# Decay attention with two expert layers on one core: another order of the steps in a chunk, and attention products in fp32

## The chip, the core and the metric

The kernel runs on one core of a Trainium2 chip. The core has five engines that run side by side, each with its own queue: TensorE (PE, matrix products; its weight loads are shown as PEld), VectorE (DVE), ScalarE (ACT), GpSimd (POOL) and SyncE (SP, which here only issues transfers). SBUF is the working memory with 128 partitions, PSUM the memory that products are written to. The metric is the device time of one execution in microseconds.

## What is computed

Three layers follow one another. The attention keeps, for each of 4 x 8 heads, a complex state of 48 x 48, which decays row by row at each of 768 steps and takes up k v. Its result goes through a dense layer of eight experts (weighted by a Sinkhorn-normalised gate) and then a layer in which each token goes to one expert.

```python
def _attn_ref(q, k, v, a_re, a_im):
    mag = np.sqrt(a_re * a_re + a_im * a_im)
    scale = np.minimum(mag, 0.999) / (mag + 1e-06)
    a_re_n, a_im_n = (a_re * scale, a_im * scale)
    for t in range(S):                      # 768 steps, B, H, D = 4, 8, 48
        ar, ai = (a_re_n[:, :, t, :, None], a_im_n[:, :, t, :, None])
        new_re = ar * S_re - ai * S_im
        new_im = ar * S_im + ai * S_re
        S_re, S_im = (new_re + k_t v_t, new_im)
        y[:, :, t] = einsum('bhd,bhde->bhe', q[:, :, t], S_re)

def _moe_ref(x, ...):   # 3072 tokens of 384; P: Sinkhorn of exp(x @ w_gate)
    for e in range(8):
        out += P[:, e:e + 1] * (np.maximum(x @ w1[e], 0.0) @ w2[e])

def _moe2_ref(x, ...):  # every token through its best expert, times the gate
    out[mask] = gate_w[mask, None] * (np.maximum(x[mask] @ w1[e], 0.0) @ w2[e])
```

## The kernel before

**Tiles.** A tile n is a chunk of 128 steps of one batch: n = chunk * 4 + batch, 24 tiles. In the attention the decays lie with (head, row) on the partitions and the steps along the free dimension, three planes of 128 steps per tile. `prep` makes the cumulated products of decays within the chunk for two tiles at once (`L = 2`; the first two tiles singly). It normalises the decays (`decay`), then scans. The 128 steps are taken as 16 runs of 8. For j = 1 to 7 step j of every run is multiplied with step j - 1: one product L233 of all four real and imaginary parts, then a difference L235 and a sum L236. Element j of all runs is a strided view, eight elements apart. Then the ends of the 16 runs are combined by doubling (L244 to L246), and these prefixes are multiplied into the other steps (L252 to L254). Squares, Ln and Exp on ACT give the inverse magnitudes, and L273 and L275 write q times the product and k over the product into `WW`.

**A tile's attention.** `stack` brings `WW` by ten transfers on SP's queue into `QK`, real part on partitions 0 to 47, imaginary part on 64 to 111. `tile_attn` makes the scores (PE, L351, fp32), masks and scales them (DVE, L355), splits them into a high and a low fp16 part (ACT L357, POOL L358), transposes K (L365, L366) and makes y of 48 fp16 products (L374): per head three with the scores and v, and from the second chunk on three with q and the state, both of which are split before (ACT L342 and L344, POOL L343, DVE L345). Powers of two for these splits come from sums of squares of q, k and v (`scales`, L303 to L317). The state is updated after U (L381): twelve small copies on ACT (L388 to L390) gather each slot's decay of the whole chunk into `C`, DVE adds the old state (L395), ACT swaps halves (L396, L397), and POOL multiplies and adds (L401 to L403).

**x.** `emit_x` scales y by a power of two from its row's largest magnitude, splits it (L421, L422), transposes it on PE (L426) and copies it to `xg` (ACT, L429). Then follow its logits (L440).

**The first two experts.** `tile_unit` runs expert 0 and 1 on pairs of tiles: zt (L506), relu and split (L527 on ACT, L528 on DVE), yt (L517), and `evac_raw` (L533 on ACT, transfer L534 on POOL's queue).

**What sets the order.** In the first phase the order on PE is written out by hand: `tile_attn` yields between its pieces and `step` puts pieces of `tile_unit` between them. The other engines' orders come from a scheduler. Products of attention share three PSUM buffers (tag "ps"), z's and zt's three, the expert outputs two. After the first phase come a dense stage on six further experts (L471, L482) and the routed stage.

## Time and profile before

| | us |
|---|---|
| runs of the kernel before | 2189.81, 2195.47, 2196.0 (median 2195.47) |
| profiled execution, span | 2188.0 |
| of it, to the first dense product after the first phase (L471) | 782.3 |
| PE busy over the span | 1962.5 (90%) |
| DVE busy over the span | 1357.6 (62%) |
| ACT busy | 903.9 (41%) |
| POOL busy | 367.1 (17%) |

The profile is one execution. Busy time is the union of an engine's instructions; an instruction may start before the one ahead of it has ended. PEclk is the granted clock of PE as a share of 2.4 GHz. "idle before" is the time in which an engine did nothing before such instructions, and after the arrow stands what ended it. The share over the whole span mixes a first phase, in which attention runs, with a long stage of plain products, so the stretches have to be read apart.

### The profile page before, as it was taken

Reading aid. Unit: us, or ns where it says so; the run is one execution under the profiler, and the core shown is the slowest. Engines: PE = TensorE matmul, PEld = TensorE weight load, DVE = VectorE, ACT = ScalarE, POOL = GpSimd, SP = SyncE. Lnnn points to the kernel's source line nnn. Section 1 sums busy time; section 2 is a strip of 40 time slices with the busy share of each in tenths; the row PEclk is TensorE's granted clock in tenths of the full one; section 3 lists DMA queues with packets and bytes.
Section 4 is the critical chain, followed back from the end, with each engine's and each line's share of the span. In section 5 each row is a group of like instructions: output and inputs, shape, how many; then the busy total and the mean of one; then the engine's idle time right before and its main releaser. Section 6 shows DMA issues by size and latency. Waiting matters only on the chain.

```text
span 2188.0 us, 37978 instructions
## 1 busy us (share of the span) xinstructions
PE 1962.5 (90%) x14770; PEld 1258.3 (58%) x14770; DVE 1357.6 (62%) x2826; ACT 903.9 (41%) x1816; POOL 367.1 (17%) x408
## 2 busy tenths in 40 slices
PE   1468878788888999999999999999999999989997
PEld 1356656666666655555555555555555555567885
DVE  8999999999996644334443443443444355554885
ACT  6565555555544433223333332433443133355111
POOL 1213332333332110000110110011011010100005
PEclk9679889999999999999999999999999999999999
DMA  4222222222222251001330231133023300143222
GB/s 159 69 81 78 80 73 81 81 81 81 81 66 73 81 189 55 29 1 58 116 116 30 87 116 58 58 116 116 29 87 116 144 25 20 38 131 130 111 89 88
DMA packets 66779, 181.53 MB, mean 83 GB/s; under 512 B 9827, under 2 KB 50799, under 8 KB 61472
## 3 DMA queue, kind: packets, MB, share of 16 engines
q0 software_dynamic: 19264, 96.19, 12.6%
q1 hardware_dynamic: 47328, 82.80, 12.6%
q8 instruction: 123, 2.02, 0.4%
q14 instruction: 64, 0.52, 0.1%
HBM read 114.09 MB, written 46.63 MB: 73 GB/s over the span
## 4 chain that ended last, share of the span: by engine, by line
PE 51%; issue 9%; POOL 1%; DMA 1%; DVE 1%; ACT 0%; POOLq 0%; SPq 0%; DVEq 0%
PE ym L482 25%; PE z L471 25%; POOL out_dram L831 1%; DMA out_dram<-ya,tok 0%; DMA late<-srt 0%; PE pt L602 0%; DVE h L528 0%; ACT h L527 0%; POOL srt L663 0%; PE pl L440 0%; PE wsum L131 0%; PE z L807 0%; DMA srt<-row,posi 0%; ACT xt L604 0%; DVE eq L627 0%
## 5 line engine op out<-in xcount | busy, mean ns | idle before, releaser
L471 PE MATMUL z<-xg,wt 128*128 128x512 f16 x2592 | 570.3, 379 | 3.5 <-ACTq L1168 3.5
L482 PE MATMUL ym<-wt,h 128*128 128x384 f16 x3456 | 572.2, 326 | 0.0
L482 PEld LDWEIGHTS <-h 128*128 128x128 f16 x3456 | 336.7, 98 | 222.3
L528 DVE SCALAR_TENSOR_TENSOR h<-z,h 128x512 f16<-128x512 f32 (+1 forms) x400 | 245.4, 615 | 300.4 <-ACT h L527 295.1
L471 PEld LDWEIGHTS <-wt 128*128 128x128 f16 x2592 | 252.0, 98 | 296.9 <-issue 1.9
L527 ACT ACTIVATE h<-z 128x512 f16<-128x512 f32 (+1 forms) x400 | 213.2, 534 | 432.2 <-PE z L471 305.5
L506 PE MATMUL zt<-xg,wt 128*128 128x256 f16 (+1 forms) x1872 | 223.5, 282 | 41.5 <-ACT xg L429 41.5
L555 DVE SCALAR_TENSOR_TENSOR acc<-ym,pf,acc 128x384 f32<-128x384 f32 x120 | 74.1, 617 | 279.1 <-PE ym L482 279.1
L517 PE MATMUL yt<-wt,ht 128*128 128x384 f16 x1152 | 210.5, 336 | 21.7 <-DVE ht L528 14.9
L506 PEld LDWEIGHTS <-wt 128*128 128x128 f16 x1872 | 183.6, 105 | 70.2 <-issue 43.1
L517 PEld LDWEIGHTS <-ht 128*128 128x128 f16 x1152 | 112.3, 102 | 106.0 <-DVE ht L528 25.7
L807 PE MATMUL z<-x,late 128*128 128x128 f16 x2016 | 131.5, 220 | 7.5 <-DVE late L796 5.1
L807 PEld LDWEIGHTS <-late 128*128 128x128 f16 x2016 | 120.9, 98 | 22.1 <-DVE late L796 6.9
L822 PE MATMUL y<-wq,h 128*128 x672 | 127.4, 327 | 1.7 <-issue 1.5
L108 ACT ACTIVATE wm<-st 128x1024 f32<-128x1024 f32 x48 | 50.7, 1057 | 145.9 <-DMA st<-in_w_dram 144.9
L358 POOL TENSOR_TENSOR sc<-sc,sc 128x512 f16<-128x512 f32 x48 | 62.9, 1311 | 173.4 <-ACT sc L357 172.4
L233 DVE TENSOR_TENSOR T<-A 128x384 f32<-128x384 f32 (+1 forms) x91 | 88.2, 969 | 2.7 <-ACT T L200 1.0
L357 ACT CAST sc<-sc 128x512 f16<-128x512 f32 x48 | 29.6, 617 | 141.7 <-DVE sc L355 141.7
L822 PEld LDWEIGHTS <-h 128*128 128x128 f16 x672 | 61.8, 98 | 33.6 <-issue 4.1
L117 ACT ACTIVATE wm<-st,ws 128x512 f16<-128x512 f32 x96 | 63.7, 713 | 38.9 <-DVE ws L138 38.9
L796 DVE COPY late<-wq 128x1536 f16 x112 | 63.0, 562 | 26.2 <-DVE ya L829 12.4
L762 POOL DMA_DIRECT2D w1d<-wm x64 | 48.0, 755 | 185.5 <-ACT wm L117 184.6
(296 smaller groups left out, 2376.2 us busy)
## 6 DMA issues: line engine op xcount, KB each, us to landing
st<-in_w_dram POOLq DMA_DIRECT2D x31, 1536.0 KB, 7.3
QK<-WW SPq DMA_DIRECT2D x96, 145.1 KB, 3.5
w1d<-wm POOLq DMA_DIRECT2D x64, 192.0 KB, 3.0
w2d<-wm POOLq DMA_DIRECT2D x32, 384.0 KB, 2.9
wq<-w2d SPq DMA_DIRECT2D x4, 3072.0 KB, 10.5
wq<-w1d SPq DMA_DIRECT2D x4, 3072.0 KB, 11.2
a<-in_att_dram SPq DMA_DIRECT2D x24, 384.0 KB, 3.8
qk<-in_att_dram SPq DMA_DIRECT2D x24, 384.0 KB, 4.3
```

The costliest lines, as they stand in the source:

```text
L117: nc.scalar.activation(hi[:, sl], st[:, sl], AF.Copy, scale=s)
L233: tt(out=x, in0=cur[:, None].to_broadcast([P, 2, 2, ns]), in1=pre[:, :, None].to_broadcast([P, 2, 2, ns]), op=ALU.mult)
L471: nc.tensor.matmul(z, w1[:, hw, k, f * P:(f + 1) * P], xg[:, hx, k, :], start=(i == 0), stop=(i == 8))
L482: nc.tensor.matmul(y, hs[f][:, hh, i * P:(i + 1) * P], w2[:, hw, f, :], start=(j == 0), stop=(j == 23))
L506: nc.tensor.matmul(z[:, f], w1[:, hw, k, o:o + P], xg[:, hx, k, :], start=(j == 0), stop=(j == 8))
L517: nc.tensor.matmul(y, hs[f // fz][:, hh, f % fz, i * P:(i + 1) * P], w2[:, hw, f, :], start=(j == 0), stop=(j == 23))
L527: nc.scalar.activation(h[:, 0], z, AF.Relu)
L528: nc.vector.scalar_tensor_tensor(out=h[:, 1], in0=z, scalar=0.0, in1=h[:, 0], op0=ALU.max, op1=ALU.subtract)
L555: self.nc.vector.scalar_tensor_tensor(out=acc, in0=y, scalar=self.pf[:, e, n:n + 1], in1=acc, op0=ALU.mult, op1=ALU.add)
L796: nc.vector.tensor_copy(wc, w1[:, bass.ds(r * 1536, 1536)])
L807: nc.tensor.matmul(z[:, f], wc[:, hw, k, f * P:(f + 1) * P], x[:, hx * 3 + k, :], start=(i == 0), stop=(i == 8))
L822: nc.tensor.matmul(y, h[:, hh, f, :], w2[:, bass.ds(r * 1536 + (hw * 2 + f) * 384, 384)], start=(i == 0), stop=(i == 5))
```

## The change

The 128 steps of a chunk are laid out anew by the host: index j * 16 + s instead of s * 8 + j, for q, k, v and the decays. In the scan, step j of all 16 runs is now one run of 16 neighbours. L233 becomes two instructions (one for each of real and imaginary part of the step before). The mask and the tokens' numbers follow the new order: `time_order` computes them once, and in the routed stage an iota per tile becomes a copy of a column of `tokid`.

The scores stay in fp32 (mask only), as do q, v and the state. So y has per head one fp32 product with the scores and one with the state; the splits, their casts and `scales` with its product fall away.

The state update is on DVE: `UV` holds U plus state and its swapped half side by side, one product with the decays straight from `QK` and one sum take the place of POOL's three instructions and ACT's twelve copies. For that, the last column of K's plane is now written as needed (imaginary part, once with its sign turned).

`emit_x` takes the power of two from the row's sum of squares: a Square with a sum on ACT and four small DVE instructions in place of a reduction and five.

The buffers `q16`, `v16`, `C`, `V`, `bound` fall away. The last pairs' decay uses the buffer `xs`.

```diff
-        v, v16, scl = self.vs.pop(n)
+        v = self.vs.pop(n)
         last = c == NC - 1
-        sc = ap.tile([P, 2, 8, P], F16, name=f"sc{n}", tag="sc")
-        if c > 0:
...
-            nc.scalar.copy(Q16[:, 0], Q[:, :, 0:128])
-            nc.gpsimd.tensor_tensor(out=Q16[:, 1], in0=Q[:, :, 0:128], in1=Q16[:, 0], op=ALU.subtract)
-            nc.scalar.activation(S16[:, 0], self.S[b], AF.Copy, scale=scl[:, 2:3])
-            nc.vector.scalar_tensor_tensor(out=S16[:, 1], in0=self.S[b], scalar=scl[:, 2:3], in1=S16[:, 0], op0=ALU.mult,
-                                           op1=ALU.subtract)
+        sc = ap.tile([P, 8, P], F32, name=f"sc{n}", tag="sc")
...
-                nc.vector.scalar_tensor_tensor(out=sc32, in0=ps, scalar=scl[:, 3:4],
-                                               in1=self.mask[:, None, :].to_broadcast([P, 4, P]), op0=ALU.mult, op1=ALU.mult)
-                nc.scalar.copy(hi, sc32)
-                nc.gpsimd.tensor_tensor(out=lo, in0=sc32, in1=hi, op=ALU.subtract)
+                tt(out=sc[:, g * 4:g * 4 + 4, :], in0=ps, in1=self.mask[:, None, :].to_broadcast([P, 4, P]), op=ALU.mult)
...
         for s in range(8):
-            parts = [(Q16, S16), (sc, v16)] if c > 0 else [(sc, v16)]
-            mm = [(l[:, i, s, :], r[:, j, cols[s]]) for l, r in parts for i, j in ((0, 0), (0, 1), (1, 0))]
-            for i, (l, r) in enumerate(mm):
-                nc.tensor.matmul(y[:, cols[s]], l, r, start=(i == 0), stop=(i == len(mm) - 1))
+            if c > 0:
+                nc.tensor.matmul(y[:, cols[s]], Q[:, s, 0:128], self.S[b][:, own[s]], start=True, stop=False)
+            nc.tensor.matmul(y[:, cols[s]], sc[:, s, :], v[:, cols[s]], start=c == 0, stop=True)
...
-            ut(out=e3(Us), in0=e3(Us), in1=Cb(0), op=ALU.mult)
-            ut(out=e3(V), in0=e3(V), in1=Cb(1), op=ALU.mult)
-            ut(out=self.S[b], in0=Us, in1=V, op=ALU.add)
+            tt(out=e4, in0=e4, in1=self.QK[n % 2][:, :, :, 128:129].to_broadcast([PR, 2, 8, 48]), op=ALU.mult)
+            tt(out=self.S[b], in0=UV[:, 0], in1=UV[:, 1], op=ALU.add)
...
-            tt(out=x, in0=cur[:, None].to_broadcast([P, 2, 2, ns]), in1=pre[:, :, None].to_broadcast([P, 2, 2, ns]),
-               op=ALU.mult)
+            x = T[:, :, :, 0:ns].rearrange("p d c (r s) -> p d c r s", s=16)
+            for d in range(2):
+                tt(out=x[:, d], in0=cur, in1=pre[:, d:d + 1].to_broadcast([P, 2, R, 16]), op=ALU.mult)
...
+        nc.scalar.activation(junk, x, AF.Square, accum_out=ss)
+        ts(out=ss, in0=ss, scalar1=2.0 ** -100, scalar2=None, op0=ALU.max)
+        ts(out=ss.bitcast(I32), in0=ss.bitcast(I32), scalar1=1, scalar2=0x7F800000, op0=ALU.logical_shift_right,
+           op1=ALU.bitwise_and)
+        ts(out=inv, in0=ss, scalar1=2.0 ** (64 - 5), scalar2=None, op0=ALU.mult)
+        nc.vector.reciprocal(out=s, in_=inv)
...
+    step = np.arange(P).reshape(16, 8).T.reshape(P)
+    st = st.reshape(4, B, 3, P, NC, P)[..., step]
```

On VectorE, the start of a pair's scan in the middle of the first phase; A are the decay products, T the scan's scratch, ht and zt belong to an expert on the tiles before. Before:

```order
L528 SCALAR_TENSOR_TENSOR ht_8_0_4089<-zt_8_0_4070,ht_8_0_4089 128x512
L233 TENSOR_TENSOR T_4358<-A_4357 128x4x96
L235 TENSOR_TENSOR A_4357<-T_4358 128x96
L236 TENSOR_TENSOR A_4357<-T_4358 128x96
L433 TENSOR_SCALAR lg<-pl_4125,invsx,wgs 128x8
```

And of the kernel after, whose lines have other numbers (L225 is L226, L232 is L233, L318 is L355):

```order
L225 TENSOR_TENSOR A_3636<-a_3634,r_3638 128x1536
L232 TENSOR_TENSOR T_3637<-A_3636 128x2x96 x2
L233 TENSOR_TENSOR A_3636<-T_3637 128x6x16
L234 TENSOR_TENSOR A_3636<-T_3637 128x6x16
L232 TENSOR_TENSOR T_3637<-A_3636 128x2x96 x2
L318 TENSOR_TENSOR sc_3340<-ps_1_3383,mask 128x512
```

One product of 4 x 96 became two of 2 x 96, and the differences and sums write whole runs of 16.

On ACT, what stands ahead of the copy of tile 11's transposed x into xg; raw is an expert's output, C the gathered decays, sc the scores of the next tile. Before:

```order
L533 COPY raw_8_4296<-yt_8_4271 128x384
L389 ACTIVATE C_160<-QK_156 48x3
L388 ACTIVATE C_160<-QK_156 48x3
L389 ACTIVATE C_160<-QK_156 48x3
L357 CAST sc_4391<-sc_0_4401 128x512
L390 ACTIVATE C_160<-QK_156 48x2 x2
L388 ACTIVATE C_160<-QK_156 48x3 x2
L389 ACTIVATE C_160<-QK_156 48x3 x2
L533 COPY raw_9_4430<-yt_9_4405 128x384
L429 COPY xg_137<-pt_4433 128x6x128
```

And of the kernel after:

```order
L347 COPY UV<-UV 48x384
L348 COPY UV<-UV 48x384
L213 ACTIVATE xs,flags<-xs 128x768
L488 COPY raw_8_3567<-yt_8_3542 128x384
L488 COPY raw_9_3697<-yt_9_3672 128x384
L384 COPY xg_151<-pt_3700 128x6x128
```

The cast of the next tile's scores and the copies of decays that stood between the two raw copies are gone.

## Rows read from the trace of the kernel before

**Rows 1.** The page's slices: busy tenths of 40 equal slices, DVE.

```profile
DVE  8999999999996644334443443443444355554885
```

**Rows 2.** Table by stretch: us; busy of PE, PEld, DVE, ACT, POOL; PEclk; DMA.

```profile
0.00:113.04 113.04, 31.83 (x253) 27.86 (x253) 102.68 (x279) 66.63 (x145) 22.81 (x33) 0.78 0.37 118
113.04:334.98 221.94, 174.40 (x1646) 138.93 (x1647) 211.56 (x392) 129.20 (x292) 67.38 (x56) 0.88 0.27 75
334.98:626.63 291.65, 240.08 (x2240) 187.59 (x2240) 281.85 (x503) 163.90 (x371) 96.85 (x81) 0.92 0.27 76
626.63:782.32 155.69, 136.43 (x1225) 101.87 (x1225) 107.76 (x252) 62.46 (x110) 32.04 (x33) 0.96 0.26 77
782.32:2188.00 1405.68, 1379.77 (x9406) 802.03 (x9405) 653.72 (x1402) 481.75 (x901) 148.04 (x207) 1.00 0.24 84
```

**Rows 3.** Timeline of DVE, 402.7 to 411.9: start, us, line, operation.

```profile
402.78 0.85 DVE L233 TENSOR_TENSOR T<-A 128x384 f32<-128x384 f32 x1
...
405.80 2.54 DVE L233 TENSOR_TENSOR T<-A 128x384 f32<-128x384 f32 x1
...
411.68 0.33 DVE L235 TENSOR_TENSOR A<-T 128x96 f32<-128x96 f32 x1
411.85 0.33 DVE L236 TENSOR_TENSOR A<-T 128x96 f32<-128x96 f32 x1
```

**Rows 4.** Timeline of POOL, the same stretch.

```profile
405.56 2.06 POOL L343 TENSOR_TENSOR q<-QK,q 128x1024 f16<-128x1024 f32 x1 [12.06 <-DMA QK<-WW]
```

**Rows 5.** Groups of DVE, 334.98 to 626.63: shapes, count, busy us, mean ns, idle before.

```profile
L233 DVE TENSOR_TENSOR T<-A 128x384 f32<-128x384 f32 x35 | 40.5, 1158 | 0.6
...
L226 DVE TENSOR_TENSOR A<-a,r 128x1536 f32<-128x1536 f32 x6 | 15.5, 2592 | 0.2
...
L235 DVE TENSOR_TENSOR A<-T 128x96 f32<-128x96 f32 x35 | 14.2, 406 | 0.8
L345 DVE SCALAR_TENSOR_TENSOR q<-S,scs,q 128x384 f16<-128x384 f32 x10 | 13.0, 1300 | 0.0
...
L309 DVE TENSOR_SCALAR sch<-sch 128x3 f32<-128x3 f32 x5 | 7.1, 1424 | 0.0
...
L269 DVE TENSOR_TENSOR T<-qk,T 128x768 f32<-128x768 f32 x5 | 4.7, 949 | 0.0
```

**Rows 6.** Undisturbed DVE operations: two groups of the first 820 us, one timeline row.

```profile
L851 DVE TENSOR_TENSOR lg<-lg,rs 128x192 f32<-128x192 f32 x8 | 2.9, 358 | 0.3
...
L269 DVE TENSOR_TENSOR T<-qk,T 128x384 f32<-128x384 f32 x2 | 1.1, 555 | 0.0
...
113.04 1.76 DVE L226 TENSOR_TENSOR A<-a,r 128x1536 f32<-128x1536 f32 x1
```

**Rows 7.** Timeline of PE, one tile: y's first and last rows, then U and yt.

```profile
393.24 0.23 PE L374 MATMUL y<-q 128*128 128x48 f16 x3 [1.25 <-ACT kt L366]
...
394.36 0.23 PE L374 MATMUL y<-v,sc 128*128 128x48 f16 x3
...
430.41 1.88 PE L381 MATMUL U<-v,kt 128*128 128x48 f32 x16
432.13 3.25 PE L517 MATMUL yt<-wt,ht 128*128 128x384 f16 x18
```

**Rows 8.** Waits of PE, 334.98 to 626.63: total us, times, longest.

```profile
PE zt L506 <- ACT xg L429: 31.3, 5, 6.3
```

**Rows 9.** Timelines of ACT and DVE, 410 to 420.

```profile
414.43 0.75 DVE L355 SCALAR_TENSOR_TENSOR sc<-ps,scs,mask 128x512 f32<-128x512 f32 x1
...
415.20 0.62 ACT L357 CAST sc<-sc 128x512 f16<-128x512 f32 x1 [4.32 <-DVE sc L355]
```

**Rows 10.** Timeline of PE after that wait.

```profile
418.27 4.00 PE L506 MATMUL zt<-xg,wt 128*128 128x256 f16 x18 [6.26 <-ACT xg L429]
...
423.08 2.13 PE L506 MATMUL zt<-xg,wt 128*128 128x256 f16 x18
```

**Rows 11.** Table by stretch, columns as in rows 2, right after the wait.

```profile
418.27:422.20 3.93, 3.93 (x19) 2.80 (x19) 3.83 (x11) 0.49 (x3) 0.10 (x1) 0.50 0.13 50
```

More of the change, by code (lines that the diff above doesn't have):

```diff
@@ L53, in consts @@
         self.mask = cp.tile([P, P], F32, name="mask")
[L54 to L55 removed]
+        self.time_order()
         self.invsx = cp.tile([P, NT], F32, name="invsx")
@@ L165, in attn_pools @@
             nc.gpsimd.memset(self.QK[i], 0.0)
-        self.C = [self.ap.tile([PR, 2, 8], F32, name=f"C{i}") for i in range(2)]
-        self.V = self.ap.tile([PR, 384], F32, name="V")
-        nc.gpsimd.memset(self.V, 0.0)
-        self.bound = [self.ap.tile([P, 1], F32, name=f"bound{i}") for i in range(2)]
-        for i in range(2):
-            nc.gpsimd.memset(self.C[i], 0.0)
-            nc.gpsimd.memset(self.bound[i], 0.0)
+        self.UV = self.ap.tile([PR, 2, 384], F32, name="UV")
+        nc.gpsimd.memset(self.UV, 0.0)
         self.S = [self.ap.tile([PR, 384], F32, name=f"S{b}") for b in range(B)]
@@ L194, in prep @@
         X = self.xs if u > 14 else spare(4 + u // 2 % 2).rearrange("p (c w) -> p c w", c=2) if u > 1 else T[:, 1]
-        return self.prep_part(u, L, a, qk, T, r, A, X, self.v2[:, k0:k0 + L], self.v16[:, :, k0:k0 + L],
-                              self.WWs[:, :, :, 3 * k0:3 * k0 + 3 * L])
+        self.vs.update((u + k, self.v2[:, k0 + k]) for k in range(L))
+        return self.prep_part(u, L, a, qk, T, r, A, X, self.WWs[:, :, :, 3 * k0:3 * k0 + 3 * L])
     def act(self, u, *args, **kw):
@@ L269, in prep_part @@
         tt(out=T1[:, 0], in0=qk[:, 1], in1=w0, op=ALU.mult)
[L270 to L274 removed]
         tt(out=WW[:, :, 1, :, 0:128], in0=t6(T1[:, 0]), in1=A6, op=ALU.mult)
[L276 removed]
+        end = lambda c: A6[:, c, :, 127]
+        self.act(u, WW[:, :, 0, :, 128], A6[:, 0:1, :, 127].to_broadcast([P, 2, R]), AF.Copy)
+        self.act(u, WW[:, 0, 1, :, 128], end(1), AF.Copy)
+        self.act(u, WW[:, 1, 1, :, 128], end(1), AF.Copy, scale=-1.0)
         self.WW.update((u + k, WW[:, :, :, 3 * k:3 * k + 3]) for k in range(L))
@@ L380, in tile_attn @@
             for s in range(8):
-                nc.tensor.matmul(U[:, cols[s]], kt[:, s, :], v[:, cols[s]], start=True, stop=True)
-            C, V = self.C[n % 2], self.V
-            z = Q[:, :, 128]
-            for half in range(2):
-                rows = slice(64 * half, 64 * half + 48)
-                for (src, cc, sg) in ((0, 0, 1.0), (64, 1, 1.0 - 2.0 * half)):
-                    s3 = z[src:src + 48]
-                    nc.scalar.activation(C[rows, cc, 0:6:2], s3[:, 0:3], AF.Copy, scale=sg)
-                    nc.scalar.activation(C[rows, cc, 1:6:2], s3[:, 3:6], AF.Copy, scale=sg)
-                    nc.scalar.activation(C[rows, cc, 6:8], s3[:, 6:8], AF.Copy, scale=sg)
@@ L391, in tile_attn @@
-            Us = ap.tile([PR, 384], F32, name=f"Us{n}", tag="Us")
+                nc.tensor.matmul(U[:, own[s]], kt[:, s, :], v[:, cols[s]], start=True, stop=True)
+            UV = self.UV
             if c == 0:
-                nc.scalar.copy(Us, U)
+                nc.scalar.copy(UV[:, 0], U)
             else:
-                tt(out=Us, in0=U, in1=self.S[b], op=ALU.add)
-            nc.scalar.copy(V[0:48], Us[64:112])
-            nc.scalar.copy(V[64:112], Us[0:48])
-            e3 = lambda t: t.rearrange("p (h e) -> p h e", e=48)
@@ L399, in tile_attn @@
-            Cb = lambda k: C[:, k, :, None].to_broadcast([PR, 8, 48])
-            ut = nc.gpsimd.tensor_tensor
-            ut(out=e3(Us), in0=e3(Us), in1=Cb(0), op=ALU.mult)
-            ut(out=e3(V), in0=e3(V), in1=Cb(1), op=ALU.mult)
-            ut(out=self.S[b], in0=Us, in1=V, op=ALU.add)
-        yield
-    def emit_x(self, n, y, back=1.0):
+                tt(out=UV[:, 0], in0=U, in1=self.S[b], op=ALU.add)
+            nc.scalar.copy(UV[0:48, 1], UV[64:112, 0])
+            nc.scalar.copy(UV[64:112, 1], UV[0:48, 0])
@@ L408, in emit_x @@
+    def emit_x(self, n, y):
         nc = self.nc
```

133 lines of the change are left out of this document (51 added, 82 removed).

## The prediction, written before the changed kernel ran

> **What bounds the kernel now.** I read the page's slices first: VectorE (DVE) is at eight tenths and mostly nine or more for the first twelve slices, about 650 us, and at about half after that [rows 1]. The table by stretch sets TensorE (PE) beside it [rows 2]. From 782 us to the end PE is busy for 1379.8 of 1405.7 us at a granted clock of 1.00. The change adds there only 24 one-column copies on GpSimd (POOL) in place of 24 iotas, so I carry this stretch over as it is. All that can move lies in the first 782 us, where attention and the first two experts run together. I cut them at the starts of tile pairs (L226 of a pair's prep): a head to 113.0, four pairs to 335.0, five pairs of almost equal length to 626.6 (291.65 us, 58.3 each), and an end to 782.3. In the five pairs DVE is busy for 281.85 of 291.65 us and PE for 240.1; in the end PE has 136.4 of 155.7. So DVE sets the pace until about 630 us. PE has an order written by hand and waits behind DVE for 51.6 us of those 291.65.
>
> **Why DVE is so slow.** The same instruction, a scan product L233 of 384 elements, takes 0.85 us at 402.78 and 2.54 us at 405.80 [rows 3]. What differs is POOL: during the second it begins the subtraction L343 at 405.56, for 2.06 us [rows 4]. In the five pairs L233's mean is 1158 ns, L226's is 2592 ns [rows 5], against 1.76 us for the L226 at 113.04 when POOL is idle [rows 6]. A tiny L309 on three elements has a mean of 1424 ns [rows 5]; it too waits for POOL.
>
> **The change, DVE per pair of tiles.** Sums are of durations; prices from [rows 5] unless said.
> - Removed: the split of the state L345, 2 x 1.30 = 2.6; the split of v L218, 1.0; the eleven small scale instructions L306 to L317, 1.42 (L309) + 0.96 (L307) + nine of about 0.17 = 3.9; in emit_x a reduction of 0.55 and five small ones become four small ones, 0.75 less per tile, 1.5; L273 twice at 1.01 becomes one product of the form of L275, at 1.76 undisturbed as in [rows 6], 0.3. Together 9.3 us.
> - Contention gone, since POOL keeps only DMA issues: L233 7 x (1.16 - 0.85) = 2.2; L235 and L236 14 x (0.43 - 0.33) = 1.4 (0.33 at 411.68 [rows 3]); L226 0.8; and about 2.6 for L275 and the other long products. Together 7.0 us.
> - Layout: the scan's operands become runs of 16 instead of single elements eight apart. A run of 192 costs 358 ns and one of 384 costs 555 ns in rows with whole runs [rows 6], about 0.16 + 0.00103 per element; so 96 elements cost 0.26 by estimate. L233 (0.85) becomes two of 0.36, L235 and L236 (0.33) become 0.26, the doubling steps gain 0.6. Together 7 x 0.13 + 14 x 0.07 + 0.6 = 2.5 us. If the runs bought nothing and only the second instruction's start were paid, it would be a loss of 7 x 0.16 = 1.1.
> - Added: the state update from POOL. Two products of 768 at 0.95 (the form of L269 in [rows 5]) and two sums of 384 at 0.555 [rows 6]: 3.0 us.
> Net: 9.3 + 7.0 + 2.5 - 3.0 = 15.8 us fewer. Durations on DVE overlap: the L236 at 411.85 starts 0.17 us after an L235 of 0.33 [rows 3]. I count nine tenths as busy time, so about 14 us go: 56.4 per pair (281.85 / 5) becomes 42 of 58.3. DVE stops being the bound. What is late next is PE.
>
> **PE per pair.** The y products change from 48 fp16 products per tile to 16 in fp32. The 48 run from 393.24 to about 394.6, 1.36 us. An fp32 product of exactly the new shape exists in the trace: U, 8 products as 16 records, 1.72 us from its start at 430.41 to the next work at 432.13 [rows 7]. So 16 cost 3.44: 2.1 us more per tile, 4.2 per pair, less 0.28 for the qkv product that falls away: +3.9. Sixteen tiles after the first four that lie before 626.6 and four in the end pay 2.1, the first four 1.0.
>
> The Trainium skill speaks against these products too: "FP8 and Floating Point Precision", section TensorE Precision Notes, gives a true fp32 product four passes. Against three fp16 products that is 4/3, so y would go from 1.36 to 1.81 us, only 0.45 more. By the row of U it is 2.1 more. By that rule alone the sum below would be some 33 us smaller (20 tiles x 1.65); the row has the same shape, so I keep the row.
>
> PE also waits less. Of the 51.6 us of waits in the five pairs, 31.3 are zt's for the transposed x, five times 6.3 [rows 8]. The chain behind one: ACT's copy L429 stands in ACT's queue behind the cast L357, which waited 4.32 us for DVE's L355 of 414.43, itself queued behind the scan [rows 9]. The cast is removed; the copy now follows only two copies of yt. What is left is the copy's 0.8 us and the way there, about 1 us per pair. The other 20 us of waits are for L366, L528 and L355, engines with a queue; with DVE at 42 of 52 us I halve them.
> There is a second gain. After the 6.26 us wait, 18 zt products take 4.00 us; the next 18 take 2.13 [rows 10]. The granted clock right after the wait is 0.50 (1.2 GHz) [rows 11]: PE had stood still for 6 us before. By 423 it is back at the higher level (2.4 GHz). Without that wait about 2 us per pair come back, and with smaller stalls a little more: 2.4.
>
> **Sums by stretch.**
> - Five pairs: 240.1 busy + 5 x 3.9 - 5 x 2.4 = 247.6, + waits 5 + 10 = 262.6. Against 291.65: **-29**.
> - Four pairs before: 174.4 + 13.5 (three with 4.2, one with 2.0, less qkv) - 7 = 181 busy; waits are 47.5 now, and 16 if they go as above: 197. Against 221.9: **-25**.
> - Head: DVE is busy for 102.7 of 113.0. It does two single tiles, one pair and the first weights. The pair gives 15, a single tile about 4 (1.9 for scales, 0.6 for v, the rest scan), together 23 of durations or 20 busy. Some of it is lost to the loads of the weights and ACT's squares, which stay. **-16**.
> - End: 136.4 + 8.4 - 2 = 142.8, waits 19.3 now, 8 then: 151. Against 155.7: **-5**.
> Sum -75: a span of 2188.0 - 75 = 2113. The median of the runs (2195.5) lies 7.5 above the span; **2120 us**. ACT loses work (24 small copies and four casts per pair among it) and gains one square per tile; at 32.8 of 58.3 us per pair (163.9 / 5, [rows 2]) it bounds nothing. POOL loses its products; the DMA issues stay. The queue of SP carries the same transfers in the same order, and the prefetch of a pair comes free when its L226 has read it, thus earlier. The new DVE state update puts two instructions between U and the next split on DVE; its reader is four tiles later, about 100 us. The square of y lengthens y's way out by one ACT instruction (0.6 us); between y and its transpose PE has U (1.72 us) and two of yt (18 of the 24 products of one take 3.25 us) [rows 7], which cover it.
>
> **Rivals.**
> *Waits half resolved.* PE's order is unchanged, so a wait can move to the next buffer: the three PSUM buffers that ps, pk, y, U, pt and pl share. Then the waits fall only to half: five pairs 253 + 26 = 279 (-12), four pairs 184 + 24 = 208 (-14), head -12, end 0: -38, **2157**. For it: in the five pairs 20 us of waits are not the x copy. Against it: these are waits on engines with a queue that gets shorter. It is also what comes out if POOL's share is not the contention that I think, with DVE near 49 busy per pair.
> *Waits stay, fp32 decides: slower.* If all 51.6 us of waits are a matter of PE's order and latency, not of DVE's load, PE pays the fp32 products on top: five pairs 247.6 to 259.6 + 51.6 = about 305 (+13), four pairs 188 + 47.5 (+13), end 144.8 + 19.3 (+8), head -16: +18, **2213**. It decides from the point where more than 291.65 - 259.6 = 32 of the 51.6 us remain. Against it: 31.3 of them hang on one cast that is gone.
> *PE runs dense.* Nearly no waits and a full clock: five pairs 252 (-39), four pairs 184 (-38), head -22, end -10: -109, **2086**. For it: PE at 782 us and later runs at 98%.
> By the four passes of the Trainium skill's page named above, the forecast's own sum would come out at 2120 - 33 = 2087, this rival's time; the row of U gives that rule little weight here.
>
> **How the numbers follow.** Forecast (2100 to 2138) 0.52, half resolved 0.25, dense 0.15, slower 0.08. The range reaches to half resolved above and to the dense case below, and takes in the layout's worse bound (1.1 + 2.5 per pair, hidden unless DVE bounds): 2084 to 2158. About 0.3%, 6.6 us, is what a measurement tells from no change. Slower by more: 0.07; within: 0.02; the rest 0.91 faster.
>
> **What would show it.** Right: DVE busy near 42 us per pair and pairs of 51 to 54 us; L233's successors at 0.36 us; no long instruction on DVE beside POOL; y at 3.5 us per tile; the wait of zt for xg at 1 us and a granted clock near 1.0 before 630 us; 782 us and later unchanged but shifted. Wrong: pairs over 56 us with PE waits above 6 us each, y products far from 216 ns, or a head that stays at 113 because the weights set it.

## The result, and the profile after

The changed kernel takes 2094.2 us (median of four runs, 2090.12 to 2094.66) against 2192.8 of the kernel before: a ratio of 0.9545, 95% interval 0.9529 to 0.956. That is 99 us faster, where 2120 was forecast. The time lies in the forecast's range (2084 to 2158) and below its own band, which ended at 2100; it is 8 us from the 2086 of the rival in which TensorE runs dense.

The slices of the page answer to [rows 1]. TensorE is at nine tenths or more from the fourth slice on. VectorE, at nine or more for most of twelve slices before, now stands at eight mostly and falls off after the tenth.

```profile
PE   2389999999999999999999999999999999989997
...
DVE  8988889888736443344434434433433455555885
```

The table by stretch (us; busy time of PE, PEld, DVE, ACT, POOL; PEclk; DMA; GB/s), cut at the same marks as [rows 2]:

```profile
0.00:104.64 104.64, 29.59 (x231) 27.11 (x231) 90.38 (x269) 52.57 (x105) 9.03 (x21) 0.80 0.39 126
104.64:289.30 184.66, 172.83 (x1503) 144.79 (x1504) 161.53 (x363) 86.51 (x162) 7.22 (x13) 0.93 0.33 91
289.30:519.35 230.05, 228.84 (x1947) 192.04 (x1945) 198.11 (x453) 103.73 (x197) 10.28 (x19) 0.99 0.36 104
519.35:685.05 165.70, 160.68 (x1310) 127.27 (x1308) 93.77 (x245) 56.30 (x106) 9.73 (x18) 0.99 0.20 61
685.05:2093.00 1407.95, 1379.02 (x9406) 800.98 (x9405) 653.49 (x1402) 481.99 (x901) 149.55 (x207) 1.00 0.24 83
```

The first phase ends at 685.05 us where it ended at 782.32, 97.3 us earlier; what follows has its old length (1407.95 against 1405.68). In the five pairs TensorE is busy for 228.8 of 230.05 us at a granted clock of 0.99, and VectorE for 198.1, so 39.6 of the 46.0 us of a pair. The stretches must be read with care: the marks are VectorE's, and VectorE now runs ahead of TensorE, so some of TensorE's work for these pairs falls into the next stretch, and the one to 685 is longer than its counterpart. Sums over the whole first phase are free of that.

TensorE's waits in the five pairs, the counterpart of [rows 8], are down to this one line (total us, times, longest):

```profile
PE zt L461 <- ACT xg L384: 1.2, 2, 0.7
```

VectorE's groups in the same stretch (shapes, count, busy us, mean ns, idle before), to be read beside [rows 5, 6]. L232 is the scan product, now two per step, L233 the difference, L225 the first product of a pair, L483 an expert's split, L289 a step of `decay`:

```profile
L483 DVE SCALAR_TENSOR_TENSOR ht<-zt,ht 128x512 f16<-128x512 f32 x38 | 26.0, 684 | 3.3 <-ACT ht L482 3.3
L232 DVE TENSOR_TENSOR T<-A 128x192 f32<-128x192 f32 x70 | 22.5, 353 | 0.6
...
L318 DVE TENSOR_TENSOR sc<-ps,mask 128x512 f32<-128x512 f32 x19 | 13.0, 687 | 2.4 <-PE ps L316 2.2
L233 DVE TENSOR_TENSOR A<-T 128x96 f32<-128x96 f32 x35 | 8.9, 255 | 0.6
...
L225 DVE TENSOR_TENSOR A<-a,r 128x1536 f32<-128x1536 f32 x5 | 8.8, 1752 | 0.0
...
L289 DVE TENSOR_SCALAR xs<-xs 128x768 f32<-128x768 f32 x4 | 2.2, 554 | 0.0
```

And TensorE's timeline over one tile's y, its first two and last two products and the work behind them (start, us), to be read beside [rows 7]. From 317.20 to the next work at 320.79 are 3.59 us for 16 products:

```profile
317.20 0.40 PE L333 MATMUL y<-S,QK 128*128 128x48 f32 x2
317.44 0.39 PE L334 MATMUL y<-v,sc 128*128 128x48 f32 x2
...
320.34 0.39 PE L333 MATMUL y<-S,QK 128*128 128x48 f32 x2
320.57 0.39 PE L334 MATMUL y<-v,sc 128*128 128x48 f32 x2
320.79 4.09 PE L461 MATMUL zt<-xg,wt 128*128 128x256 f16 x36
```

Before, y's 48 fp16 products began at 393.24, and the next work came 1.20 us later:

```profile
394.44 4.09 PE L506 MATMUL zt<-xg,wt 128*128 128x256 f16 x36
```

### The profile page after: what moved, and what is told of

Its sections match the earlier page's. It is cut to its first block, busy times and chain, and to the rows that moved or that the text cites. A ratio compares the mean times of both kernels' runs of the same rounds, so it can differ in the third digit from the quotient of the medians.

```text
span 2093.0 us, 36448 instructions
## 1 busy us (share of the span) xinstructions
PE 1971.0 (94%) x14392; PEld 1292.2 (62%) x14392; DVE 1197.3 (57%) x2727; ACT 781.1 (37%) x1471; POOL 185.8 (9%) x278
## 4 chain that ended last, share of the span: by engine, by line
PE 52%; issue 10%; POOL 1%; DVE 1%; DMA 1%; ACT 1%; POOLq 0%; SPq 0%; DVEq 0%; ACTq 0%
PE ym L437 26%; PE z L426 26%; POOL out_dram L786 1%; DMA late<-srt 1%; DMA st<-in_w_dram 0%; PE pt L557 0%; ACT h L482 0%; DVE h L483 0%; DVE wt L137 0%; PE pl L395 0%; POOL srt L618 0%; PE wsum L150 0%; DMA srt<-row,posi 0%; ACT wt L127 0%; DVE acc L510 0%
## 5 line engine op out<-in xcount | busy, mean ns | idle before, releaser
L426 PEld LDWEIGHTS <-wt 128*128 128x128 f16 x2592 | 252.2, 98 | 297.5 <-issue 2.7
L483 DVE SCALAR_TENSOR_TENSOR h<-z,h 128x512 f16<-128x512 f32 (+1 forms) x400 | 245.4, 615 | 300.1 <-ACT h L482 294.1
L461 PE MATMUL zt<-xg,wt 128*128 128x256 f16 (+1 forms) x1872 | 208.8, 271 | 2.3 <-ACT xg L384 2.3
L472 PE MATMUL yt<-wt,ht 128*128 128x384 f16 x1152 | 197.7, 329 | 0.0
L461 PEld LDWEIGHTS <-wt 128*128 128x128 f16 x1872 | 177.4, 102 | 24.2 <-issue 3.6
L482 ACT ACTIVATE ht<-zt 128x512 f16<-128x512 f32 x96 | 57.1, 595 | 123.2 <-PE zt L461 123.1
L316 PE MATMUL ps<-QK 128*128 128x128 f32 x384 | 56.0, 292 | 27.4 <-DMA QK<-WW 27.0
L489 POOL DMA_DIRECT2D rawd<-raw x48 | 26.2, 545 | 600.2 <-ACT raw L488 600.2
L483 DVE SCALAR_TENSOR_TENSOR ht<-zt,ht 128x512 f16<-128x512 f32 x96 | 65.8, 685 | 19.4 <-ACT ht L482 18.9
## 6 DMA issues: line engine op xcount, KB each, us to landing
QK<-WW SPq DMA_DIRECT2D x96, 145.1 KB, 3.4
```

The lines of the kernel that those rows point to most:

```text
L316: nc.tensor.matmul(ps[:, j, :], K[:, h, 0:128], Q[:, h, 0:128], start=True, stop=True)
L426: nc.tensor.matmul(z, w1[:, hw, k, f * P:(f + 1) * P], xg[:, hx, k, :], start=(i == 0), stop=(i == 8))
L461: nc.tensor.matmul(z[:, f], w1[:, hw, k, o:o + P], xg[:, hx, k, :], start=(j == 0), stop=(j == 8))
L472: nc.tensor.matmul(y, hs[f // fz][:, hh, f % fz, i * P:(i + 1) * P], w2[:, hw, f, :], start=(j == 0), stop=(j == 23))
L482: nc.scalar.activation(h[:, 0], z, AF.Relu)
L483: nc.vector.scalar_tensor_tensor(out=h[:, 1], in0=z, scalar=0.0, in1=h[:, 0], op0=ALU.max, op1=ALU.subtract)
```

## The experiments

My theory was that POOL's reading stretched VectorE and that VectorE's load set the pace before, and that TensorE sets it now, with VectorE having 6.4 us per pair to spare. The kernels in this table test it. All ratios are to the kernel before, timed beside them. Its median was 2189.9 to 2192.8 us in these sets, so two medians of this table can be compared to some 3 us, and ratios are the better measure of small differences.

| run | median us | ratio | 95% interval |
|---|---|---|---|
| changed kernel | 2094.2 | 0.9545 | 0.9529 to 0.956 |
| e1_pool_extra | 2163.0 | 0.9874 | 0.9854 to 0.9895 |
| e2_pool_memset | 2098.1 | 0.9572 | 0.9554 to 0.9589 |
| e2_dve14 | 2190.4 | 0.9989 | 0.9979 to 0.9998 |
| e1_uv_pool | 2092.7 | 0.9556 | 0.954 to 0.9572 |
| e3_before_uv | 2179.8 | 0.9951 | 0.9932 to 0.997 |
| e1_strided | 2105.7 | 0.9611 | 0.9592 to 0.963 |
| e1_before_layout | 2156.3 | 0.9849 | 0.9832 to 0.9865 |
| e2_no_qs | 2057.5 | 0.9382 | 0.9366 to 0.9398 |
| e2_scv16 | 2072.4 | 0.9451 | 0.9435 to 0.9467 |
| e3_w_early | 2085.4 | 0.9521 | 0.9504 to 0.9537 |
| e3_w_early_order | 2088.6 | 0.9541 | 0.9521 to 0.9561 |
| e3_best | 2083.6 | 0.9515 | 0.95 to 0.9529 |

### Does POOL stretch VectorE? (e1_pool_extra, e2_pool_memset)

```diff
+        if c > 0:
...
+            ut(out=px, in0=Q[:, :, 0:128], in1=px, op=ALU.subtract)
...
+                ut(out=px, in0=sc[:, g * 4:g * 4 + 4, :], in1=px, op=ALU.subtract)
...
+            for k in range(2):
+                ut(out=pu, in0=pu, in1=self.QK[n % 2][:, k, :, 128:129].to_broadcast([PR, 8, 48]), op=ALU.mult)
+            ut(out=self.pu, in0=self.pu, in1=self.S[b], op=ALU.add)
```

> The changed kernel, with POOL's instructions added back in number and size (per tile one of 1024 elements, two of 512, three of 384); they read what their models read and write buffers of their own that nobody reads. Theory (POOL stretched VectorE's instructions before, and TensorE sets the pace now): the 192-element scan product rises from 0.36 us to a mean above 0.42, the 1536-element product from 1.75 to above 2.2, VectorE's busy time per pair from 39.6 to 45 to 48 us, about the 46.0 us that a pair takes, so the time rises by 5 to 25 us over 2094. Rival A (the long instructions of before came from the strided operands, not from POOL): 0.36 and 1.75 us stay, time within 3 us of 2094. Rival B (TensorE's waits come back as a whole once VectorE is stretched): 50 us or more.

It took 2163.0 us, 69 more than the changed kernel: nearly seven tenths of the whole gain is given back by POOL instructions whose results nobody reads. The stretch of five pairs (columns as above):

```profile
319.07:580.23 261.16, 241.53 (x1906) 198.09 (x1906) 241.42 (x453) 101.31 (x194) 94.73 (x75) 0.93 0.31 89
```

VectorE's groups in it (shapes, count, busy us, mean ns, idle before):

```profile
L236 DVE TENSOR_TENSOR T<-A 128x192 f32<-128x192 f32 x70 | 38.5, 580 | 0.6
L497 DVE SCALAR_TENSOR_TENSOR ht<-zt,ht 128x512 f16<-128x512 f32 x38 | 26.0, 685 | 4.9 <-ACT ht L496 4.7
...
L326 DVE TENSOR_TENSOR sc<-ps,mask 128x512 f32<-128x512 f32 x18 | 12.3, 682 | 1.0 <-PE ps L324 1.0
...
L272 DVE TENSOR_TENSOR WW<-T,A 128x1536 f32<-128x1536 f32 x5 | 11.6, 2313 | 0.0
...
L293 DVE TENSOR_SCALAR xs<-xs 128x768 f32<-128x768 f32 x4 | 4.1, 1018 | 0.0
```

TensorE's longest wait there (total us, times, longest):

```profile
PE zt L475 <- ACT xg L398: 9.2, 3, 3.8
```

The product of 192 elements (L236) goes from 353 to 580 ns, the one of 1536 (L272) from 1752 to 2313. L497 and L326, which take one of their inputs from PSUM, stay at 685 and 682 (684 and 687 in the changed kernel). So products with both inputs in SBUF suffer, and an instruction with one of two inputs in PSUM does not. The Trainium skill says this in "SBUF — State Buffer", section Who interferes with whom: a DVE instruction with two SBUF inputs contends with a GpSimd instruction that reads SBUF. These rows agree. Products with two inputs are not all: L293, a tensor_scalar with a single input in SBUF, goes from 554 (L289) to 1018 ns too. VectorE's load rises to 48.3 us per pair (241.42 / 5), and a pair takes 52.2. My price for that was too low (5 to 25 us): I had VectorE reach the length of a pair and stop there, but the pair became 3.9 us longer than VectorE's load, TensorE waited again and its clock fell to 0.93, and the head, where VectorE is busy for nearly nine tenths, took 8.3 more. The time is the one of Rival B (50 us or more), its reason only in part: of the 51.6 us for which TensorE stood in the five pairs of the kernel before, 19.6 came back (261.16 less 241.53), not all.

The second run fills a buffer on POOL instead, reading nothing:

```diff
+        fill = lambda k: [nc.gpsimd.memset(self.px, 0.0) for _ in range(k)]
```

> In place of POOL's added instructions of the first run the same places hold plain fills (memsets) of a buffer of their own, eleven of 768 elements per tile at 0.84 us (the duration of the fill of UV in the trace), so POOL is busy as long, some 9 us per tile, but reads nothing. Theory (it is POOL's reading that stretches VectorE): the 192-element product stays at 0.36 us, the time within 4 us of 2094. Rival (any busy POOL does it): 2150 or more, as with the instructions that read.

2098.1 us, 4 more than the changed kernel (6 by the ratios, whose intervals overlap). The fills wait for nothing and so ran ahead of their tiles, all before 290 us; the stretch to compare is 105.6 to 290, where POOL is busy for 113 of 184 us. The stretch of e2_pool_memset:

```profile
105.56:290.04 184.48, 174.48 (x1543) 147.85 (x1543) 161.90 (x363) 87.56 (x166) 113.39 (x157) 0.94 0.32 89
```

The scan product in it stands at 354 ns:

```profile
L233 DVE TENSOR_TENSOR T<-A 128x192 f32<-128x192 f32 x56 | 18.0, 354 | 0.7
```

In e1_pool_extra, with reading instructions on POOL, it took 443 in the same four pairs:

```profile
L236 DVE TENSOR_TENSOR T<-A 128x192 f32<-128x192 f32 x56 | 22.9, 443 | 0.7
```

So for products with two inputs in SBUF it is POOL's reading that counts, as the same section of the Trainium skill has it (they do not contend with an instruction that only writes), and not POOL being busy. For a tensor_scalar that is not so: the one of 768 elements, 0.55 us alone, took twice as long at 101.88 (1.11 us) and at 190.94, in the midst of fills, though not at 147.62 (0.56), where fills ran as well:

```profile
190.94 1.02 DVE L290 TENSOR_SCALAR xg<-xg 128x768 f32<-128x768 f32 x1
```

### Is it VectorE's load that made TensorE wait? (e2_dve14)

```diff
+            if u > 1 and j <= 7:
+                for _ in range(2):
+                    tt(out=self.dj, in0=self.dj, in1=self.dj, op=ALU.mult)
```

> The changed kernel with 14 more VectorE products of 768 elements (0.955 us each by the trace) in each pair's scan, 13.4 us per pair, nobody reads them, no POOL beside. Theory (a pair takes the longer of VectorE's load, with a little on top, and TensorE's): 39.6 + 13.4 = 53 busy, pairs of 54 to 55.5 us, 11 pairs, 85 to 105 us slower: 2180 to 2200, and TensorE's waits and its lower clock are back. Rival (before was slow by POOL's latency in chains and not by load): far less, 30 to 60 us, since no chain waits for these products.

2190.4 us, 96 more: the whole gain is gone, without POOL and without a chain that waits for these products. They too ran ahead: 108 of the 154 lie in five pairs from 139.7 to 441.9, seven behind these. In the five VectorE is busy for 57.4 us of each pair's 60.4. The two stretches:

```profile
139.74:441.91 302.17, 239.05 (x2056) 201.36 (x2056) 287.06 (x565) 105.40 (x202) 9.75 (x18) 0.89 0.24 70
441.91:620.42 178.51, 172.35 (x1430) 143.71 (x1431) 160.42 (x361) 76.98 (x147) 7.78 (x14) 0.95 0.35 103
```

TensorE's wait in the first of them is one alone, in front of the scores, five times (the first of the five began before the stretch, so the sum is above the 63.1 us for which TensorE stands in it):

```profile
PE ps L321 <- DMA QK<-WW: 70.9, 5, 18.7
```

After 441.9 four pairs take 178.5 us, 44.6 each. So a pair takes what the fuller of the two engines needs, and a little on top where that is VectorE (60.4 for 57.4). Because the load was not spread evenly as I had expected, the agreement of the total (85 to 105 forecast) says less than the two stretches.

### The state update (e1_uv_pool, e3_before_uv)

Undone in the changed kernel, and done alone in the kernel before:

```diff
-            tt(out=e4, in0=e4, in1=self.QK[n % 2][:, :, :, 128:129].to_broadcast([PR, 2, 8, 48]), op=ALU.mult)
-            tt(out=self.S[b], in0=UV[:, 0], in1=UV[:, 1], op=ALU.add)
+            ut = nc.gpsimd.tensor_tensor
+            ut(out=e4, in0=e4, in1=self.QK[n % 2][:, :, :, 128:129].to_broadcast([PR, 2, 8, 48]), op=ALU.mult)
+            ut(out=self.S[b], in0=UV[:, 0], in1=UV[:, 1], op=ALU.add)
```

```diff
-            ut = nc.gpsimd.tensor_tensor
+            ut = nc.vector.tensor_tensor
```

> The state update's product and sum back on POOL, all else as in the changed kernel. Theory (TensorE sets the pace, VectorE has 46.0 - 39.6 = 6.4 us to spare per pair): VectorE loses 3.0 us per pair and gains 1 to 3 by being stretched beside POOL; time within 4 us of 2094. Rival (the move to VectorE is a main part of the gain): 15 us or more slower, with waits of TensorE in the pairs.

> In the kernel before, the state update's three instructions (L401 to L403) on VectorE in place of POOL, nothing else. VectorE gets 3 x about 0.58 us per tile, 3.5 per pair; POOL loses 4.25 of its 9.2 us of products per tile, so by theory nearly half of the stretching (7 to 9 us per pair) goes, 3 to 4 us: about even, 2193 within 12 us. Rival A (the update's way over POOL was the wait): 25 us or more faster. Rival B (only load counts, there is no stretching): 3.5 x 11 = 35 us slower.

The first took 2092.7 us, no difference. VectorE's load is 40.4 us per pair (201.77 / 5) where it was 39.6: what POOL's two instructions stretch takes back what they save. The scan product in that stretch, with POOL's larger instruction (L351, 1671 ns each) beside it:

```profile
L232 DVE TENSOR_TENSOR T<-A 128x192 f32<-128x192 f32 x70 | 25.7, 396 | 0.8
```

The second took 2179.8, about 10 us faster than the kernel before beside it (0.9951): within the 12 us of "about even" by that measure, 13 by the 2193 that was named, and well short of Rival A's 25. TensorE's waits change places there (kt is K transposed, ht an expert's split relu output). The wait for the transposed x, 31.3 us in [rows 8], is down to 2.6, but others have grown (before: y for kt 6.3, yt for ht 6.1):

```profile
PE yt L517 <- DVE ht L528: 11.5, 5, 2.6
PE y L374 <- ACT kt L366: 11.1, 10, 1.8
PE ps L351 <- DMA QK<-WW: 7.7, 5, 2.4
PE y L374 <- POOL sc L358: 5.6, 5, 1.1
...
PE zt L506 <- ACT xg L429: 2.6, 3, 1.5
```

The five pairs of that run:

```profile
342.84:627.74 284.90, 243.80 (x2240) 191.82 (x2240) 275.33 (x533) 164.25 (x367) 67.80 (x50) 0.93 0.28 77
```

TensorE stands for 41.1 us there, where it stood for 51.6: the one wait lost 28.7 us, all together 10.5. The wait named in a row is thus not a cost that goes with the row: as long as VectorE is full (275.33 of 284.90 us), others take most of its place.

### The layout (e1_strided, e1_before_layout)

```diff
-            cur, pre = A5[:, :, :, j], A5[:, :, :, j - 1]
+            cur, pre = A3[:, :, :, j], A3[:, :, :, j - 1]
...
-    step = np.arange(P).reshape(16, 8).T.reshape(P)
+    step = np.arange(P)
```

That is e1_strided, with A3 the old view of single elements eight apart. The other run is the reverse edit in the kernel before: the new order of steps, scan, mask and tokens, nothing else.

> The layout alone undone: steps in their old order, the scan's operands eight elements apart, one product of 4 x 96 per step. Theory: VectorE's busy time per pair rises by 2 to 4 us to 42 to 44, still below 46.0, so the time stays within 5 us of 2094. Rival (the layout is a main part of the gain): 11 pairs times 2.5 to 4 us, 25 to 45 us slower.

> The layout alone put into the kernel before. Theory (VectorE sets the pace there): 2.5 to 4 us per pair less on VectorE, times 11 pairs, nine tenths of it: 25 to 40 us faster than 2193, that is 2153 to 2168. Rival (the pairs of before were set by chains of latency between engines, not by VectorE's load): within 7 us of 2193.

In the kernel before the layout alone brings 35 us (2191.1 to 2156.3). Taken out of the changed kernel it costs 11.5 by the medians (2105.7) and 14 by the ratios. The load on VectorE moves by like amounts: per pair from 56.4 to 52.1 there (260.54 / 5), from 39.6 to 42.6 here (213.15 / 5). Only the 3.0 us here are a clean price. Beside POOL's instructions the new layout also changes which of VectorE's are stretched: the state's split (L345 in [rows 5]), which the layout does not touch, falls from 13.0 to 6.1 us and the first product from 15.5 to 10.5, while the products of 630 elements rise from 15.4 to 23.9. The 35 us are thus what the layout was worth in that kernel, and not a price of strides. Five pairs of e1_before_layout:

```profile
325.24:594.02 268.78, 240.34 (x2274) 191.89 (x2271) 260.54 (x539) 162.97 (x372) 90.40 (x80) 0.94 0.29 82
```

And the first product of a pair there:

```profile
L245 DVE TENSOR_TENSOR A<-a,r 128x1536 f32<-128x1536 f32 x6 | 10.5, 1749 | 0.0
```

The head and the five pairs of e1_strided:

```profile
0.00:111.22 111.22, 34.23 (x231) 29.80 (x231) 94.39 (x246) 53.09 (x105) 9.11 (x21) 0.77 0.37 119
...
293.29:528.24 234.95, 231.67 (x1928) 192.57 (x1926) 213.15 (x416) 102.27 (x195) 10.30 (x19) 0.97 0.34 98
```

Its scan product of 384 elements, eight apart, takes 0.857 us where two of 192 in runs take 0.706:

```profile
L231 DVE TENSOR_TENSOR T<-A 128x384 f32<-128x384 f32 x35 | 30.0, 857 | 0.8
```

I had expected at most 5 us in e1_strided. The nine pairs do give only 2.3 (417.0 against 414.7 us). But 6.6 of the rest lie in the head (111.2 against 104.6), where VectorE is busy for 94.4 and 90.4 us, 85 and 86%; my theory had left the head out.

### What fp32 costs TensorE (e2_no_qs, e2_scv16)

```diff
-            if c > 0:
-                nc.tensor.matmul(y[:, cols[s]], Q[:, s, 0:128], self.S[b][:, own[s]], start=True, stop=False)
```

```diff
-                tt(out=sc[:, g * 4:g * 4 + 4, :], in0=ps, in1=self.mask[:, None, :].to_broadcast([P, 4, P]), op=ALU.mult)
+                tt(out=sc32, in0=ps, in1=self.mask[:, None, :].to_broadcast([P, 4, P]), op=ALU.mult)
+                nc.scalar.copy(hi, sc32)
+                tt(out=lo, in0=sc32, in1=hi, op=ALU.subtract)
...
-            nc.tensor.matmul(y[:, cols[s]], sc[:, s, :], v[:, cols[s]], start=c == 0, stop=True)
+            for i, (p, r) in enumerate(((0, 0), (0, 1), (1, 0))):
+                nc.tensor.matmul(y[:, cols[s]], sc[:, p, s, :], v16[:, r, cols[s]], start=c == 0 and i == 0, stop=i == 2)
```

> Leaves out the product of q with the state, so y holds only the chunk's own steps. Theory (TensorE sets the pace outside the head): eight fp32 products less in 20 tiles at 1.72 us each, 34 us less in the first phase, 31 to 36 by the time: 2058 to 2064. Rival (VectorE or waits set it): 0 to 15 us less.

> The product of scores and v back to three fp16 products per head (without scales), the rest as in the changed kernel: per tile TensorE loses 8 x (0.215 - 3 x 0.028) = 1.05 us, VectorE gains two differences of 512 and half of one of 768, about 1.9, ACT two casts. Theory (fp32 products cost TensorE time, VectorE has 6.4 us per pair to spare outside the head): 24 x 1.05 = 25 less in the pairs and the end, 3 to 6 more in the head: 2072 to 2080. Rival (the splits' way from the scores over VectorE and ACT to y makes waits again): 2094 or more.

Both came out as TensorE's time says. Without the product with the state the time falls by 36 us (0.9545 to 0.9382 of the kernel before), TensorE's time for y by 36. With fp16 products for scores and v the time falls by 21 (0.9545 to 0.9451), TensorE's time for y by 26. The table of the instructions of tile y alone, over the whole first phase; first the kernel before (us; busy PE, DVE, ACT; it shows no PEld):

```profile
0.00:782.32 782.32, 34.50 (x1056) 27.87 (x48) 13.88 (x24) 0.90 0.28 82
```

The changed kernel (busy PE, PEld, DVE, ACT):

```profile
0.00:685.05 685.05, 83.26 (x704) 81.00 (x704) 14.74 (x24) 27.83 (x72) 0.95 0.32 93
```

e2_no_qs:

```profile
0.00:644.72 644.72, 46.91 (x384) 44.71 (x384) 14.75 (x24) 27.74 (x72) 0.95 0.34 99
```

e2_scv16:

```profile
0.00:659.71 659.71, 57.47 (x896) 47.75 (x320) 14.69 (x24) 27.70 (x72) 0.95 0.33 97
```

VectorE's extra work in e2_scv16 (43.3 us per pair, 216.62 / 5) is covered, as expected. In its five pairs TensorE does not stand at all, beside a VectorE that is busy for 96% of them, though the scores are split again ahead of y (by a cast on ACT and a difference on VectorE):

```profile
283.35:509.39 226.04, 226.04 (x2097) 187.59 (x2095) 216.62 (x485) 120.74 (x226) 10.81 (x20) 1.00 0.35 100
```

It is the fastest of these kernels with the whole computation, 2072.4 us: keeping the scores in fp32 was a loss, hidden in a gain nearly five times as large.

### The head (e3_w_early, e3_w_early_order, e3_best)

In the changed kernel TensorE stands for 21 us from 88.7 for the sum of squares of a weight matrix, whose load waited for a buffer. Then it waits for the transfers into QK that the scores of tile 2 need. Its timeline:

```profile
109.62 0.59 PE L150 MATMUL wsum<-wss,ones 128*128 128x3 f32 x2 [20.96 <-ACT wt L127]
...
112.43 2.08 PE L316 MATMUL ps<-QK 128*128 128x128 f32 x8 [1.56 <-DMA QK<-WW]
```

e3_w_early loads that matrix at the start into two buffers that are free until tile 8:

```diff
+                halves = [self.xg[g].rearrange("p a k t -> p (a k t)").bitcast(F32) for g in (2, 3)]
-                early = chain(*(self.wprep("", e, self.wts[e], self.wsc, stage if e == 0 else (None, None), True)
+                early = chain(*(self.wprep("", e, self.wts[e], self.wsc, stage if e == 0 else (None, halves), True)
```

e3_w_early_order also moves expert 0's work on tile 1 ahead of the scores of tile 2 in the order by hand (the moved part, put on one line each: t2 is a piece of tile 2's attention, e a piece of an expert's work on a tile), and e3_best adds the fp16 products of e2_scv16:

```diff
-  x1 t2 p A1 e w t2 w p x1 e t2 t2 w w p x2
+  x1 p A1 e w w p x1 w t2 t2 e t2 t2 w w p x2
```

> The changed kernel; the second matrix of expert 1 is loaded at the program's start into the xg buffers of groups 2 and 3, which are free until tile 8, so its sum of squares no longer waits for st. In the changed kernel TensorE stands at that sum from 88.7 to 109.6 us. Theory (the next in TensorE's order is the score product of tile 2, whose QK comes only at 112.4 after VectorE's head work, with nothing in between but the transposes of tile 1): the wait moves there, gain 0 to 4 us, 2090 to 2094. Rival (the load is what holds the head): 12 to 20 us faster, 2074 to 2082.

> As e3_w_early, and in the hand-written order expert 0 on tile 1 (zt, zt, yt: about 3 + 2.2 + 4 us of TensorE) is put ahead of the scores of tile 2. Theory: this work now lies in the 20 us in which TensorE stood, VectorE's two splits of ht delay the scores of tile 2 by 1.4: 6 to 10 us faster than the changed kernel, 2084 to 2088. Rival (VectorE's head work is the only bound, what TensorE does there buys nothing): within 2 us of e3_w_early.

> e3_w_early_order together with the fp16 products of scores and v of e2_scv16. Theory: the two gains lie in different stretches (head; pairs and end) and add: 2072.4 - 6 to 10 = 2062 to 2066. Rival (VectorE, now with 43 us per pair and a longer head, takes one of them back): 2070 or more.

TensorE's timeline in e3_w_early, the sum of squares and the scores of tile 2:

```profile
87.57 0.35 PE L164 MATMUL wsum<-wss,ones 128*128 128x3 f32 x2
...
108.13 2.08 PE L330 MATMUL ps<-QK 128*128 128x128 f32 x8 [18.54 <-DMA QK<-WW]
```

In e3_w_early_order, expert 0's work and the scores:

```profile
90.27 6.64 PE L475 MATMUL zt<-xg,wt 128*128 128x128 f16 x72 [0.89 <-ACT xg L398]
...
110.02 3.75 PE L330 MATMUL ps<-QK 128*128 128x128 f32 x16 [8.98 <-DMA QK<-WW]
```

In e3_best, the scores:

```profile
120.54 3.79 PE L342 MATMUL ps<-QK 128*128 128x128 f32 x16 [21.50 <-DMA QK<-WW]
```

In e3_w_early the wait moved to the scores, as expected, yet they came 4.3 us earlier than I had assumed. VectorE finished their input at almost the same time (its last product into WW began at 100.39 in the changed kernel, here at 99.68), but the transfers into QK took less, now that the weights' load no longer runs beside them. Issues in 95 to 115 us of the changed kernel (count, KB, median us to landing):

```profile
QK<-WW SPq DMA_DIRECT2D x7, 145.1 KB, 5.5
```

And of e3_w_early:

```profile
QK<-WW SPq DMA_DIRECT2D x8, 145.1 KB, 3.4
```

The share of time in which the DMA engines are busy agrees: 0.92 and 0.99 in 100 to 104 and 104 to 108 us of the changed kernel, 0.84 and 0.52 here. But the load need not be the whole cause: for tile 1, at 60 to 76 us, such transfers took 5.1 and 3.8 us with no weight load beside them in either run. The time fell to 0.9521, 5 us better than the changed kernel by ratios and below the 2090 to 2094 expected, though the intervals overlap a little. In e3_w_early_order TensorE does 10.9 us more before 108 (41.4 busy against 30.6), and none of it is left at the end (0.9541). The scores of tile 2 come 1.9 us later, and after them TensorE waits for QK again (3.1 and 2.4 us), for xt (1.7) and ht (0.9): VectorE, busy for some nine tenths until 200 us, has the next tiles ready no earlier. In e3_best the scores of tile 2 come at 120.5, and the sum (0.9515) is worse than e2_scv16 alone (0.9451), where 2062 to 2066 us had been expected. VectorE's last product into WW begins at 111.70 there, and at 101.36 in e3_w_early_order. The added splits are only some of these 10 us: between the first product of that pair and the last VectorE also does four more weight splits (ten, not six) and four instructions of the next pair's `decay`, 3 us each together, since the scheduler's order came out otherwise. So e3_best does not show what the two gains are worth in another order. The rivals were nearer the truth here: the head is mostly VectorE's, and work moved earlier on TensorE is given back. e3_w_early with the fp16 products, without the new order, was not tried.

## Why the prediction was right or wrong, step by step

**What bounds.** Right: VectorE's load set the pace until 630 us, TensorE sets it behind the head now (228.8 of 230.05 us). e2_dve14 shows it from the one side, e2_no_qs from the other.

**VectorE per pair.** 42 us were forecast, 39.6 came. The prices held: 0.353 us for a product of 192 (0.36), 0.255 for 96 elements (0.26), 1.75 for the long ones (1.76). POOL's contention, put at 7.0 us per pair, measures 8.7 when it is put back (39.6 to 48.3). The layout, put at 2.5, measures 3.0 in the changed kernel; the 4.3 in the one before hold the changed stretching of other instructions. One reading was a little off: L343 on POOL had begun 0.24 us ahead of the slow L233, not during it, and the two then ran side by side. The update in exchange for less contention was rightly nearly even. Whether removing the splits and small scale instructions saved 9.3 was not tried by itself.

**TensorE's fp32 products.** Right: 3.44 us per tile by the row of U, 3.59 measured, in all 48.8 us more for y (34.5 to 83.3) where the terms made 46. The 1.36 us taken off for fp16 run to the end of the last product; counted to the next work, as for U, they are 1.20, so a tile pays 2.4 and not 2.1. The four passes of the Trainium skill ("FP8 and Floating Point Precision", section TensorE Precision Notes) would by estimate have made it 1.81 per tile; no run here shows that for these short products, and the 3.59 decide. That the total came near the 2087 of that rule is an accident of another term.

**TensorE's waits: the term that was mis-sized most.** The sum kept 39 us of waits in pairs and end (16 + 15 + 8); there are 18.1 (11.8 + 1.2 + 5.0 by the stretches that answer to [rows 2], 172.83 of 184.66, 228.84 of 230.05, 160.68 of 165.70), and 5 of the 11.8 are the end of the head's wait for a weight matrix (to 109.62). "With DVE at 42 of 52 us I halve them" was the wrong reading: in the five pairs the waits did not halve, they went from 51.6 to 1.2 us, and in e2_scv16 to nothing beside a VectorE at 96%. That VectorE, no longer the fuller engine, runs ahead of TensorE is seen in the marks; that its load and not the shorter chains did it is shown by e2_dve14, where load alone brings waits back, and by e2_scv16, which puts casts and splits back without any. The rival of a dense TensorE had this right.

**The clock.** Same sign, too small. TensorE's busy time in the first phase was 582.7 and would be 628 with y and without the qkv products (3.4); it is 591.9. So by what is left over 36 us came back with the higher clock, where I had 21 (2.4 x 5, 7 and 2). The products that both kernels do in the same number (zt 223.5 to 208.7 us, yt 210.5 to 197.7, ps 60.3 to 56.0, pk 22.7 to 21.8) take 33 us less, which agrees. The granted clock in the five pairs is 0.99, was 0.92.

**The head.** -16 was forecast, -8.4 came. It lost 12 us of VectorE's work (102.7 to 90.4), and the loads of the weights stayed: TensorE stands for 75 of 104.6 us. By e1_strided and e3_w_early_order VectorE sets most of the pace there still.

**Together** the span is 20 us below the forecast's 2113: busy time 11 lower (clock), waits in pairs and end 21 lower, the head's idle time some 10 higher, the stretch after 2 higher. The rest of the 26 is the step from the span to the median: I carried 7.5 us over from one profiled run, and here it is 1.2. (The profiled run of before itself took 2189.81, 1.8 over its span; the other 5.7 were the spread of three runs.)

**The rivals.** *PE runs dense*, given 0.15, came nearest. The marks have moved, so only the sum of pairs and end can be compared: 669.3 us before, 580.4 now, 582 by that rival and 611 by the forecast. It missed the head (-22 against -8.4) as the forecast did. That the range held the result is owed to its lower edge, which was drawn at this rival; the forecast's own mechanism explains the direction and two thirds of what the pairs and the end gained. *Waits half resolved*: e2_dve14 and e1_pool_extra show what it needs, VectorE near the pair's length. *Waits stay*: against it stands the single line of waits above. Its reasoning, that fp32 costs TensorE on top, was true by 49 us.

**Not settled.** The row scales from sums of squares were not tried alone, nor fp16 products for q and the state in the changed kernel. They would stand in for products that take 36 us in fp32, and by estimate take 12 themselves (480 at 0.025 us), but add splits to VectorE.
